# A grouped expert kernel on one core: half a unit of a visit between ScalarE's copies and the routing matmuls that read them

## The chip, the cores and the metric

The kernel runs on one core of a Trainium2 chip. Its engines are PE (TensorE, matmuls and transposes), DVE (VectorE), ACT (ScalarE), POOL (GpSimd) and SP (SyncE, which here only issues transfers). The metric is the device time of one execution in microseconds, as the median of several runs; less is better.

## The reference

A causal convolution over 7 positions with weights from a softmax makes the token rows; these are routed, by two small matmuls and two argmax, to one of 16 experts (4 groups of 4), and each token's row goes through its expert.

```python
w = softmax(weight_gen)                                # (8, 2880, 8, 7)
x = einsum('bshk,bskhg->bshg', w, windows_of(x))       # (8, 2880, 192), then 23040 rows
g_logits = x @ w_group                                 # (23040, 4)
g_idx = argmax(g_logits, axis=1); g_w = softmax(g_logits)[g_idx]
...
e_logits = xg @ w_expert[g]                            # (n, 4)
e_idx = argmax(e_logits, axis=1); e_w = softmax(e_logits)[e_idx]
...
h = maximum(xg[mask_e] @ w1[g, e], 0.0)                # 192 -> 1024
out[tok_idx] = (g_w * e_w)[:, None] * (h @ w2[g, e])   # 1024 -> 192
```

The functions `softmax` and `windows_of` stand here for the lines that the reference writes out.

## The kernel before

**Two streams in one program.** The 23040 tokens lie as 128 partitions by 180 columns, in 15 groups of 12 columns, counted from 0. The first stream makes groups: DVE convolves a group in two chunks of 6 columns (multiplications L317, additions L335), and then the group is routed. The second stream visits experts: a visit takes 128 or 256 rows of one expert through its two matmuls. Rows go from the first stream to the second through a buffer in memory: POOL scatters a group's token rows to places sorted by expert (L532, twelve scatters of 128 rows each, tensor `rows`), and SP loads a visit's rows from there (L823, tile `xb`).

**Rounds.** The visits are made in 14 rounds. Round 0 runs after groups 0 and 1, as ten short "plain" visits. Each later round r may run as soon as group r + 1 is scattered and its table of visits is made. Visits 10 to 13 belong to round 1, 14 to 18 to round 2, 19 to 25 to round 3. So visit 19 is the first that needs rows of group 4, and SP's load of its rows waits until all scatters of group 4 have landed. The last round needs the last group, 14.

**Units.** A visit is cut into units (eight hidden blocks of 128 are two in a unit). In a unit PE runs `gemm1` of that unit (L959, inputs `xh` and `xl`, weights `wa`), then `gemm2` (L1005) of the unit two before, as LAG = 2. In the first unit of a visit the next visit's rows are prepared: ScalarE copies a part of them (`xd`, L915), and in its second unit PE transposes them (tile `tpx`, L933 and L934; plain visits L922, tile `tp`) between gemm1 and gemm2; ScalarE then copies `xh` and DVE subtracts for `xl` (L890). DVE splits the weights too (`wa`, L890 as well). Units are counted here through the whole program: unit 2 is early in the plain visits, and visit 19's input transposes stand in unit 74.

**Routing a group** (`logits`, then `ranks`). ScalarE copies a part of a chunk (`rem`, L411). For each pair of columns PE makes three transposes (L418, L418, L419), and ScalarE copies them to `xT` (L424). After three pairs of each of the two chunks PE computes the scores (L401, sixteen matmuls), ScalarE copies them (L431), PE turns them (L436, the "logits' turns") and ScalarE copies `ls` (L439). DVE then finds the largest, PE counts ranks by two matmuls (L476, L477), DVE takes them over (`pre`, L487) and makes positions (`posi`, L507). For groups 2 and later POOL copies each column of posi to one of three small tiles `ix` (L531) and scatters (L532). POOL also scatters a visit's results to `out` (L1043, tiles `y`), in the one order of its instructions.

**What sets the order.** Python code writes the instructions in one order, with a clock for each engine (`clk`) that it advances by estimated costs; nothing is reordered later. The visits' loop (`blocks`) emits a unit and then calls `fill`, which lets the first stream emit steps until DVE's clock is far enough. Steps of the routing generators are taken by `move`. A generator that yields NEXT is not taken further within the unit (there is an exception in a hurry), and one that yields UNIT not before the count of gemm units has gone up. `pause(t)` yields UNIT only where the visits have begun and the copy's estimated end t lies more than 0.9 us behind PE's clock; else NEXT, after which a hurrying generator goes on in the same unit.

Of the kernel before, what the change touches and what calls it, by code (L numbers as in the profile page):

```python
# [42 lines left out]
def conv_moe_kernel(ctx: ExitStack, tc: tile.TileContext, x, wgen, w_group, w_expert, w1, w2, out):  # L43
# [205 lines left out]
        spare[name].append(spare[name].pop(0))  # L249
        return spare[name][-1]  # L250

    state = {"slots": False, "open": False, "unit": 0, "starve": False, "begun": False, "gemm": 0, "ph": 0, "hold": False}

    def ph_tile(k, shape):
        return ps_h.tile(shape, F32, name=f"ph{k}")
# [17 lines left out]
        def __init__(self, o, n):  # L273
            self.o, self.n = o, n

    NEXT, UNIT = object(), object()

    def round_of(g):
        return next(r for r in range(NR) if g < ENDS[r])
# [107 lines left out]
    def logits(g, o):  # L387
        n = WIDTHS[g]
        xrow = o.xrow
        early = g < FIRST  # L390
        pause = lambda t: UNIT if state["begun"] and t > clk["pe"] + 0.9 else NEXT
        yield Chunk(o, 1)
        new_lt = lambda: ps_y.tile([P, SG // 4, P], F32, name="py0") if g == FIRST - 1 else ps_l.tile([P, SG // 4, P], F32, name="pl")
        lt = new_lt() if early else None

        xTs = rt.tile([P, SG // 4, 2, 3, P], F32, name="xT")

        def score(q0, q1):
            for u in range(2):
                for j in range(4):  # L400
                    nc.tensor.matmul(  # L401
                        lt[j * LW:(j + 1) * LW, q0:q1, :], lhsT=wr[:, u * (1 + j % 2), :], rhs=xTs[:, q0:q1, j // 2, (j % 2, 2)[u], :],
                        start=u == 0, stop=u == 1, tile_position=(0, j * LW))

        txTs, scored = [], 0
        for s2 in range(0, n, 2):
            if o.chunks <= s2 // SC:
                yield Chunk(o, s2 // SC + 1)
            if s2 % SC == 0:
                rem = rt.tile([P, SC, HP], F32, name="rem")  # L410
                nc.scalar.copy(out=rem, in_=xrow[s2 // SC][:, :, P:D])  # L411
                txTs += [run("act", 0.4, clk["dve"])] * 2
                yield pause(txTs[-1])
            ttp = run("pe", 0.35, txTs[-2])
            tp = ps_t.tile([P, 3, P], F32, name="tp") if s2 % 4 == 0 else ph_tile(0, [P, 3, P]) if early else ps_l.tile([P, SG // 4, P], F32, name="pl")
            row = xrow[s2 // SC][:, s2 % SC:s2 % SC + 2, :]
            for u in range(2):
                nc.tensor.transpose(out=tp[:, u, :], in_=row[:, u, 0:P], identity=ident)  # L418
            nc.tensor.transpose(out=tp[:, 2, :], in_=rem[:, s2 % SC:s2 % SC + 2, :].rearrange("p s d -> p (s d)"), identity=ident)  # L419
            if early and s2 == 4:  # L420
                run("pe", 0.5, txTs[-1])
                score(0, 1)
                scored = 1
            nc.scalar.copy(out=xTs[:, s2 // 4, s2 % 4 // 2], in_=tp)  # L424
            txTs.append(run("act", 0.48, ttp))
            yield NEXT if s2 < n - 2 else pause(txTs[-1])
        lt = lt or new_lt()
        run("pe", 0.1 + 0.4 * (n // 4 - scored), txTs[-1])
        score(scored, n // 4)
        lts = xTs[:, 0].rearrange("p w u t -> p (w u) t")[:, 0:3, :]  # L430
        nc.scalar.copy(out=lts, in_=lt)  # L431
        tlt = run("act", 0.48, clk["pe"])
        yield pause(tlt)
        lp = ps_l.tile([P, SG // 4, P], F32, name="pl")
        for u in range(n // 4):
            nc.tensor.transpose(out=lp[:, u, :], in_=lts[:, u, :], identity=ident)  # L436
        run("pe", 0.35, tlt)
        ls = rt.tile([P, SG, NL], F32, name="ls")[:, 0:n, :]
        nc.scalar.copy(out=ls, in_=lp.rearrange("p q (j l) -> p (q j) l", l=LW)[:, 0:n, 0:NL])  # L439
        run("act", 0.4, clk["pe"])  # L440
        ranking.append([ranks(g, o, ls, Until(clk["act"] + LATE[0 if early else 1])), None])
# [301 lines left out]
    def move(qs, q, most):  # L743
        for _ in range(most):
            if q[1] is not None:
                what, v = q[1]
                if what == "time" and v > clk["dve"] or what == "unit" and v == state["unit"] and most < HURRY or what == "gemm" and v == state["gemm"] or what == "chunk" and (v.o.chunks < v.n or state["hold"] and v.n > 1):
                    return
                q[1] = None
            c = next(q[0], None)  # L750
# [3 lines left out]
            if c is NEXT:  # L754
                q[1] = "unit", state["unit"]
            elif c is UNIT:
                q[1] = "gemm", state["gemm"]
            elif isinstance(c, Chunk):
                q[1] = "chunk", c
            elif isinstance(c, Until):  # L760
                q[1] = "time", c
            else:
                yield c
# [3 lines left out]
    def step():  # L767
# [7 lines left out]
        if state["starve"] or not state["slots"] and c is NEXT:  # L775
            state["unit"] += 1
            state["gemm"] += state["starve"]
        return c

    def fill(until):  # L780
# [289 lines left out]
    def blocks(n0, n1, paced):  # L1070
# [99 lines left out]
        for i in range(len(units) + LAG):  # L1170
            if i < len(units):
# [14 lines left out]
                if u == last and i + 1 < len(units):  # L1186
                    cur = nxt
            asks = []
            if i >= LAG:
                b, u = queue.pop(0)  # L1190
                gemm2(b, u)
# [6 lines left out]
            if i < len(units):  # L1198
# [19 lines left out]
                    did += 1  # L1218
                state["unit"] += 1
                state["gemm"] += 1  # L1220
            flush()
            if paced:
                fill(clk["pe"] + AHEAD[0 if cur.plain else 1 if cur.o.whole else 2])
# [48 lines left out]
```

## Time and profile before

| what | value |
| --- | --- |
| median of 3 runs | 1158.08 us (1158.06 to 1162.09) |
| profiled execution | 1155.21 us |
| its span | 1153.2 us |
| PE busy | 1097.4 us, 95% |
| DVE busy | 950.2 us, 82% |
| ACT busy | 648.8 us, 56% |
| POOL busy | 583.9 us, 51% |
| moved by transfers | 275.06 MB, mean 239 GB/s |

The span is what the profiler saw between the first and the last instruction; the execution around it is 2.0 us longer, and it lies 2.9 us below the median of the other runs. A busy time is a sum over the span. An engine with less than all of it waits somewhere, and the timelines say for whom: in brackets behind an instruction stands the idle time just before it and what ended that.

### The profile page before, as it was taken

The page shows a single profiled execution, that of the slowest core. Times are in us where ns is not written, and L with a number is a line of the kernel's source. Part 1 is how long each engine was busy: PE and PEld are TensorE (multiplying, and loading weights), DVE is VectorE, ACT ScalarE, POOL GpSimd, SP SyncE. Part 2 cuts the span into 40 slices and gives each one's busy share as a digit, 9 for nine tenths or more (in the row PEclk, how much of TensorE's full clock was granted, in tenths as well). Part 3 has the DMA queues.
Part 4 walks back from the last instruction along what each step waited for, and adds up shares of the span by engine and source line. Part 5 has one row for each costly group of instructions (what it writes and reads, how often), then busy time and mean ns, then how long its engine had stood idle before and what let it go on. Part 6 is the DMA issues. An engine that isn't in the chain of part 4 may idle for free.

```text
span 1153.2 us, 23883 instructions
## 1 busy us (share of the span) xinstructions
PE 1097.4 (95%) x7909; PEld 1028.1 (89%) x7909; DVE 950.2 (82%) x1682; ACT 648.8 (56%) x1307; POOL 583.9 (51%) x613
## 2 busy tenths in 40 slices
PE   4777998999999999999999999999999999999997
PEld 2444888999999999999999999999999899999997
DVE  8899997989998999999899989899674676665661
ACT  1341444655656565565565655655656676667762
POOL 7065185738267574757484747375657321222211
PEclk9998999999999999999999999999999999999999
DMA  6798899986877887978797878875769885666562
GB/s 178 211 318 232 288 308 305 271 279 204 296 238 227 274 294 216 284 247 287 224 298 230 275 235 239 287 236 180 220 203 272 248 250 162 177 199 199 164 218 65
DMA packets 84342, 275.06 MB, mean 239 GB/s; under 512 B 15296, under 2 KB 34160, under 8 KB 82416
## 3 DMA queue, kind: packets, MB, share of 16 engines
q1 hardware_dynamic: 64056, 229.77, 64.1%
q0 software_dynamic: 20032, 43.39, 12.3%
q8 instruction: 64, 1.05, 0.4%
q14 instruction: 70, 0.57, 0.1%
q10 hardware_dynamic: 120, 0.28, 0.1%
HBM read 225.83 MB, written 47.88 MB: 237 GB/s over the span
## 4 chain that ended last, share of the span: by engine, by line
PE 73%; issue 8%; DMA 6%; DVE 6%; POOL 4%; ACT 2%; SPq 0%; POOLq 0%; DVEq 0%; ACTq 0%
PE ph L959 31%; PE py L1005 26%; PE py L1007 3%; DVE pr L317 3%; DMA raw<-in_moe_w 2%; POOL rows L532 2%; DMA xin<-in_x 2%; PE py L1008 2%; POOL out L1043 2%; PE pl L401 1%; PE tpx L934 1%; DMA xb<-rows 1%; PE tpx L933 1%; PE ph L358 1%; PE pl L1016 1%
## 5 line engine op out<-in xcount | busy, mean ns | idle before, releaser
L959 PE MATMUL ph<-xh,wa 128*128 128x256 f32 (+3 forms) x1992 | 450.6, 301 | 0.0
L1043 POOL DMA_INDIRECT out<-y,xb x189 | 217.7, 1152 | 392.3 <-DVE y L1038 164.7
L1005 PE MATMUL py<-wc,hh 128*128 128x192 f32 x2160 | 399.1, 326 | 0.0
L959 PE MATMUL ph<-xl,wa 128*128 128x256 f32 (+3 forms) x1328 | 349.8, 284 | 0.6 <-DVE xl L890 0.6
L1005 PEld LDWEIGHTS py<-wc,hh 128*128 128x128 f32 x2160 | 344.9, 189 | 0.2
L959 PEld LDWEIGHTS ph<-xh,wa 128*128 128x128 f32 x1992 | 334.2, 189 | 8.4 <-issue 8.4
L968 ACT ACTIVATE hh<-ph 128x512 f32<-128x512 f32 (+2 forms) x296 | 165.7, 560 | 252.0 <-PE ph L959 250.8
L317 DVE TENSOR_TENSOR pr<-xin,wt 128x1152 f32<-128x1152 f32 x186 | 249.0, 1350 | 4.1 <-PE py L358 3.6
L959 PEld LDWEIGHTS ph<-xl,wa 128*128 128x128 f32 x1328 | 250.7, 189 | 1.0 <-DVE xl L890 0.9
L532 POOL DMA_INDIRECT rows<-xrow,ix x156 | 222.8, 1428 | 45.8 <-POOL ix L531 34.9
L335 DVE TENSOR_TENSOR xrow<-xrow,pr 128x1152 f32<-128x1152 f32 x144 | 194.7, 1352 | 0.7
L890 DVE SCALAR_TENSOR_TENSOR pr<-ph,hh 128x256 fp32r<-128x256 f32 (+2 forms) x128 | 65.7, 513 | 81.2 <-ACT hh L973 43.1
L890 DVE TENSOR_TENSOR wa<-raw,wa 128x1024 fp32r<-128x1024 f32 x83 | 101.3, 1220 | 19.4 <-ACT wa L866 19.2
L531 POOL COPY ix<-posi 128x1 int32<-128x1 int32 x156 | 73.5, 482 | 68.3 <-DMA rows<-xrow,ix 38.3
L1007 PE MATMUL py<-wc,hh 128*128 128x384 f32 x320 | 101.1, 361 | 0.0
L973 ACT ACTIVATE hh<-ph 128x256 fp32r<-128x256 f32 (+2 forms) x128 | 59.1, 462 | 53.7 <-PE ph L959 53.6
L866 ACT CAST wa<-raw 128x1024 fp32r<-128x1024 f32 x83 | 87.1, 1050 | 0.0
L875 ACT CAST wa<-raw 128x1024 fp32r<-128x1024 f32 x83 | 86.5, 1042 | 0.0
L1008 PE MATMUL py<-wc,pr 128*128 128x192 f32 x320 | 80.1, 250 | 0.0
L1032 ACT ACTIVATE y<-py,xb 128x192 f32<-128x192 f32 x175 | 66.2, 426 | 21.1 <-PE py L1005 19.4
L890 DVE TENSOR_TENSOR xl<-tpx,xh 128x512 fp32r<-128x512 f32 (+1 forms) x83 | 56.4, 680 | 14.3 <-ACT xh L939 14.0
L1008 PEld LDWEIGHTS py<-wc,pr 128*128 128x128 f32 x320 | 60.9, 190 | 0.0
(205 smaller groups left out, 1315.6 us busy)
## 6 DMA issues: line engine op xcount, KB each, us to landing
wc<-in_moe_w SPq DMA_DIRECT2D x73, 768.0 KB, 6.5
raw<-in_moe_w SPq DMA_DIRECT2D x83, 512.0 KB, 6.1
xin<-in_x SPq DMA_DIRECT2D x14, 1728.0 KB, 10.8
raw<-in_moe_w SPq DMA_DIRECT2D x91, 256.0 KB, 5.2
raw<-w1lo SPq DMA_DIRECT2D x83, 256.0 KB, 5.2
xb<-rows SPq DMA_DIRECT2D x75, 194.0 KB, 5.1
wa<-in_moe_w SPq DMA_DIRECT2D x24, 384.0 KB, 6.7
raw<-in_moe_w SPq DMA_DIRECT2D x11, 768.0 KB, 8.6
```

What stands on the lines that cost most here:

```text
L317: nc.vector.tensor_tensor(out=dst, in0=o.xin[:, c0 + k:c0 + k + SC, :].rearrange("p s (h g) -> p s h g", g=HG), in1=w4[:, c0:c0 + SC, :, k ...
L335: nc.vector.tensor_tensor(out=acc, in0=acc, in1=prs[k - 2], op=ALU.add)
L532: written_once(nc.gpsimd.indirect_dma_start(out=rows[:, :], out_offset=bass.IndirectOffsetOnAxis(ap=ix, axis=0), in_=src, in_offset=None, ...
L866: nc.scalar.copy(out=o.wa[:, 0, :], in_=o.raw[0])
L875: nc.scalar.copy(out=o.wa[:, 2, :], in_=o.raw[1])
L890: f(*a, **k)
L959: nc.tensor.matmul(ph[:, v, :], lhsT=w[:, f0:f0 + P], rhs=rhs, start=i == 0, stop=i == len(terms) - 1)
L968: nc.scalar.activation(out=hh, in_=ph, func=AF.Relu)
L1005: nc.tensor.matmul(b.acc[t], lhsT=hh[:, v, c], rhs=wc[0][:, f, :], start=f == 0 and not (b.wide and t == 1), stop=f == NFT - 1 and not (b. ...
L1007: nc.tensor.matmul(b.py[t], lhsT=hh[:, v, c], rhs=wc[f // 4][:, f % 4].rearrange("p l d -> p (l d)"), start=f == 0, stop=False)
L1008: nc.tensor.matmul(b.acc[t], lhsT=hl[:, v, c], rhs=wc[f // 4][:, f % 4, 0, :], start=False, stop=f == NFT - 1)
L1043: ins = nc.gpsimd.indirect_dma_start(out=out[:, :], out_offset=bass.IndirectOffsetOnAxis(ap=b.x.bitcast(I32)[part, t, D + 1:D + 2], axis=0 ...
```

## The change

Between gemm1 and gemm2 of a unit there is now a point at which a routing generator can go on. A new count, `half`, goes up at that point and again at the unit's end; a generator that yields HALFWAY isn't taken further until the count has gone up. `brief(t)` yields HALFWAY for groups below MAIN + 3 = 6, if the visits have begun, and for the last group; for others it is `pause(t)` as before. It stands in two places: after the last transposes, before the scores, and after the scores, before the turns. If a generator waits for a half, `fill` is called at the new point as well.

```diff
@@ -249,7 +249,7 @@
-    state = {"slots": False, "open": False, "unit": 0, "starve": False, "begun": False, "gemm": 0, "ph": 0, "hold": False}
+    state = {"slots": False, "open": False, "unit": 0, "starve": False, "begun": False, "gemm": 0, "half": 0, "ph": 0, "hold": False}
@@ -273,7 +273,7 @@
-    NEXT, UNIT = object(), object()
+    NEXT, UNIT, HALFWAY = object(), object(), object()
@@ -389,6 +389,7 @@
         pause = lambda t: UNIT if state["begun"] and t > clk["pe"] + 0.9 else NEXT
+        brief = lambda t: HALFWAY if state["begun"] and (g < MAIN + 3 or g + 1 == ENDS[-1]) else pause(t)
@@ -423,14 +424,14 @@
             txTs.append(run("act", 0.48, ttp))
-            yield NEXT if s2 < n - 2 else pause(txTs[-1])
+            yield NEXT if s2 < n - 2 else brief(txTs[-1])
         lt = lt or new_lt()
         run("pe", 0.1 + 0.4 * (n // 4 - scored), txTs[-1])
         score(scored, n // 4)
         lts = xTs[:, 0].rearrange("p w u t -> p (w u) t")[:, 0:3, :]
         nc.scalar.copy(out=lts, in_=lt)
         tlt = run("act", 0.48, clk["pe"])
-        yield pause(tlt)
+        yield brief(tlt)
@@ -744,7 +745,7 @@
-                if what == "time" and v > clk["dve"] or what == "unit" and v == state["unit"] and most < HURRY or what == "gemm" and v == state["gemm"] or what == "chunk" and (v.o.chunks < v.n or state["hold"] and v.n > 1):
+                if what == "time" and v > clk["dve"] or what == "unit" and v == state["unit"] and most < HURRY or what == "gemm" and v == state["gemm"] or what == "half" and v == state["half"] or what == "chunk" and (v.o.chunks < v.n or state["hold"] and v.n > 1):
@@ -755,6 +756,8 @@
             elif c is UNIT:
                 q[1] = "gemm", state["gemm"]
+            elif c is HALFWAY:
+                q[1] = "half", state["half"]
@@ -775,6 +778,7 @@
             state["gemm"] += state["starve"]
+            state["half"] += state["starve"]
@@ -1186,6 +1190,9 @@
             asks = []
+            state["half"] += 1
+            if paced and any(q[1] and q[1][0] == "half" for q in scoring):
+                fill(clk["pe"] + AHEAD[0 if cur.plain else 1 if cur.o.whole else 2])
             if i >= LAG:
@@ -1218,6 +1225,7 @@
                 state["gemm"] += 1
+                state["half"] += 1
```

Below is what stands in a row on three engines. The changed kernel's line numbers are a few higher (L401 is L402, L436 is L437, L959 is L963, L1005 is L1009, L890 is L894, L531 is L532, L532 is L533, L1043 is L1047).

On PE, group 4's second chunk. Before, in unit 52: the end of a gemm2, the transposes (`xrow`, `rem`), the scores into `pl`, the turns, then the next gemm1:

```order
L1005 MATMUL py_2429<-wc,hh 128x192
L418 MATMUL pl<-ident,xrow 128x128 x2
L419 MATMUL pl<-ident,rem 128x128
L418 MATMUL tp<-ident,xrow 128x128 x2
L419 MATMUL tp<-ident,rem 128x128
L418 MATMUL pl<-ident,xrow 128x128 x2
L419 MATMUL pl<-ident,rem 128x128
L401 MATMUL pl<-xT,wr 32x384 x8
L436 MATMUL pl<-ident,xT 128x128 x3
L959 MATMUL ph_2503<-xh_181,wa 128x256 x2
```

After, from the last transposes of unit 54 to the first matmuls of unit 56:

```order
L419 MATMUL pl<-ident,xrow 128x128 x2
L420 MATMUL pl<-ident,rem 128x128
...
L963 MATMUL ph_2561<-xh_181,wa 128x256
L963 MATMUL ph_2561<-xl_183,wa 128x256
L402 MATMUL pl<-xT,wr 32x384 x8
L1009 MATMUL py_2586<-wc,hh 128x192
L1009 MATMUL py_2587<-wc,hh 128x192
L1009 MATMUL py_2586<-wc,hh 128x192
L1009 MATMUL py_2587<-wc,hh 128x192
L437 MATMUL pl<-ident,xT 128x128 x3
L963 MATMUL ph_2611<-xh_181,wa 128x256 x2
```

The transposes stand two units later, in a unit that also holds a visit's input transposes; a gemm1 has moved between them and the scores, and a gemm2 between the scores and the turns. Groups 2, 3 and 14 change in the same way: the second transposes of 2 and 14 stay in their unit (2 and 271), those of 3 go from 27 to 28, and the scores of each stand behind the next unit's gemm1. Group 4's rank matmuls move from unit 57 to 60, those of group 2 from 10 to 11, of group 3 from 33 to 35, of group 14 from 274 to 276. In group 5, which already had a gemm2 between its transposes and its scores in unit 77, the scores move ahead of that gemm2, and the turns from unit 78 to the end of 77; its first transposes move from unit 66, which holds input transposes, to 67. Group 4's first transposes move from unit 43 to 46, which holds input transposes.

On DVE, the same group from the ranks to the positions. Before:

```order
L335 TENSOR_TENSOR xrow<-xrow,pr 128x6x192
L317 TENSOR_TENSOR pr<-xin,wt 128x1152
L487 COPY pre<-pl 128x16x11
...
L501 TENSOR_TENSOR sel<-sel,oh 128x192
L890 TENSOR_TENSOR wa<-raw_193,wa 128x1024
L890 TENSOR_TENSOR xl_183<-tpx,xh_181 128x2x256
L504 TENSOR_REDUCE pos<-sel 128x12
L507 SCALAR_TENSOR_TENSOR posi<-pos 128x12
```

After:

```order
L894 TENSOR_TENSOR wa<-raw_193,wa 128x1024
L894 TENSOR_TENSOR xl_183<-tpx,xh_181 128x2x256
...
L335 TENSOR_TENSOR xrow<-xrow,pr 128x6x192 x2
L288 TENSOR_REDUCE m<-wt 128x96
L290 TENSOR_TENSOR wt<-wt,m 128x672
L488 COPY pre<-pl 128x16x11
...
L502 TENSOR_TENSOR sel<-sel,oh 128x192
L505 TENSOR_REDUCE pos<-sel 128x12
L508 SCALAR_TENSOR_TENSOR posi<-pos 128x12
```

The subtractions wa and xl have left the middle of the chain and stand ahead of it; the pair of additions and two operations of the next softmax, which stood behind posi, are ahead of `pre` now. In the last group wa and xl move from before `pre` to a place earlier still, ahead of the group's second argmax.

On POOL, the same group's scatters. Before, an out scatter and the first rows of the chain, whose twelve scatters have nothing between them:

```order
L1043 DMA out<-y_187,xb 23040x192
L531 COPY ix_177<-posi 128x1
L531 COPY ix_178<-posi 128x1
L531 COPY ix_176<-posi 128x1
L532 DMA rows<-xrow,ix_177 188928x194
L532 DMA rows<-xrow,ix_178 188928x194
L532 DMA rows<-xrow,ix_176 188928x194
L531 COPY ix_177<-posi 128x1
L532 DMA rows<-xrow,ix_177 188928x194
```

After, from the third scatter on:

```order
L533 DMA rows<-xrow,ix_176 188928x194
L532 COPY ix_177<-posi 128x1
L1047 DMA out<-y_188,xb 23040x192
L533 DMA rows<-xrow,ix_177 188928x194
L532 COPY ix_178<-posi 128x1
L532 COPY ix_176<-posi 128x1
L1047 DMA out<-y_189,xb 23040x192
L533 DMA rows<-xrow,ix_178 188928x194
L533 DMA rows<-xrow,ix_176 188928x194
```

Two out scatters that stood behind the chain stand inside it. On SP two row loads move: visit 14's stands behind a weight load (`wc`) that it stood ahead of, and visit 19's behind three (`raw`).

## Rows read from the trace of the kernel before

**Rows 1.** The page: busy time of the engines, share of the span, instructions.

```profile
PE 1097.4 (95%) x7909; PEld 1028.1 (89%) x7909; DVE 950.2 (82%) x1682; ACT 648.8 (56%) x1307; POOL 583.9 (51%) x613
```

**Rows 2.** Stretch 165 to 215 us: busy time, clock, DMA share, GB/s.

```profile
165.00:215.00 50.00, 44.41 (x335) 41.05 (x334) 42.86 (x80) 26.95 (x57) 31.99 (x32) 1.00 1.03 317
```

**Rows 3.** Waits of PE, 105 to 300 us: total us, times, longest us.

```profile
PE pl L436 <- ACT xT L431: 1.8, 3, 0.6
PE pl L401 <- ACT xT L424: 1.7, 3, 0.6
PE tp L922 <- DMA xb<-rows: 1.7, 1, 1.7
...
PE tpx L933 <- DMA xb<-rows: 1.3, 1, 1.3
```

**Rows 4.** Timeline of PE, group 4: start, us, operation, [idle before <-releaser].

```profile
229.58 0.44 PE L418 MATMUL pl<-ident,xrow 128*128 128x128 f32 x2 [0.24 <-ACT xT L424]
...
230.69 1.50 PE L401 MATMUL pl<-xT,wr 128*32 128x384 f32 x16 [0.57 <-ACT xT L424]
232.79 0.55 PE L436 MATMUL pl<-ident,xT 128*128 128x128 f32 x3 [0.60 <-ACT xT L431]
```

**Rows 5.** Waits of PE, 820 to 930 us.

```profile
PE tpx L933 <- DMA xb<-rows: 1.2, 2, 0.9
PE pl L436 <- ACT xT L431: 0.6, 1, 0.6
PE pl L401 <- ACT xT L424: 0.6, 1, 0.6
```

**Rows 6.** Timeline of PE, 245 to 291 us: ranks, two units, transposes, v19.

```profile
245.92 0.25 PE L476 MATMUL pl<-oh,tri 128*128 128x192 bf16 x1
...
246.03 0.48 PE L959 MATMUL ph<-xh,wa 128*128 128x256 f32 x2
...
253.84 0.54 PE L959 MATMUL ph<-xh,wa 128*128 128x256 f32 x2
...
271.73 0.44 PE L418 MATMUL tp<-ident,xrow 128*128 128x128 f32 x2 [1.17 <-ACT xT L424]
...
290.96 0.27 PE L933 MATMUL tpx<-ident,xb 128*128 128x128 f32 x1
```

**Rows 7.** Timeline of DVE, group 4's positions and the convolution behind them.

```profile
250.33 0.17 DVE L507 SCALAR_TENSOR_TENSOR posi<-pos 128x12 int32<-128x12 f32 x1
...
253.74 2.75 DVE L335 TENSOR_TENSOR xrow<-xrow,pr 128x1152 f32<-128x1152 f32 x2
```

**Rows 8.** Timeline of POOL: an out scatter, then group 4's chain.

```profile
250.87 0.98 POOL L1043 DMA_INDIRECT out<-y,xb  x1 [0.30 <-ACT wa L875]
...
254.99 0.97 POOL L532 DMA_INDIRECT rows<-xrow,ix  x1 [0.30 <-issue]
258.21 1.11 POOL L531 COPY ix<-posi 128x1 int32<-128x1 int32 x1 [2.25 <-DMA rows<-xrow,ix]
...
278.96 1.80 POOL L532 DMA_INDIRECT rows<-xrow,ix  x1 [0.28 <-POOL ix L531]
```

**Rows 9.** Timeline of SP: the row load of visit 19.

```profile
283.73 0.33 SPq L823 DMA_DIRECT2D xb<-rows  x1
```

**Rows 10.** Timeline of PE, last group: ranks, unit 277, first stalled visit.

```profile
845.14 0.25 PE L476 MATMUL pl<-oh,tri 128*128 128x192 bf16 x1
...
850.12 0.42 PE L959 MATMUL ph<-xh,wa 128*128 128x256 f32 x1
...
895.66 0.33 PE L933 MATMUL tpx<-ident,xb 128*128 128x128 f32 x1 [0.85 <-DMA xb<-rows]
```

**Rows 11.** Timeline of DVE, last group: from the ranks to the positions.

```profile
848.93 0.33 DVE L487 COPY pre<-pl 128x176 f32<-128x176 f32 x1
...
851.35 0.17 DVE L507 SCALAR_TENSOR_TENSOR posi<-pos 128x12 int32<-128x12 f32 x1
```

**Rows 12.** Timeline of SP: the load that PE waits for at 895.66.

```profile
893.29 0.33 SPq L823 DMA_DIRECT2D xb<-rows  x1
```
## The prediction

> **What bounds the kernel now.** I read the page first, then the windows, PE's waits, and the timelines around each wait. The page shows PE busy for 95% of the span [rows 1], so only time in which PE stands still can be won, and each such time has a releaser. In the list of PE's waits between 105 and 300 us the reader is to see two pairs: the scores (L401) wait three times for ScalarE's copy L424, the logits' turns (L436) three times for the copy L431 [rows 3]. These are groups 2, 3 and 4 (counted from 0); the timeline of group 4 shows one pair, 0.57 and 0.60 us [rows 4]. The last group pays it once more [rows 5]. The other waits in these lists are for rows that come back from memory (xb) [rows 3, 5]. Between 165 and 215 us the DMA engines are booked for 1.03 of the time and PE's granted clock is 1.00 [rows 2], so PE's time lost there is lost to transfers.
>
> **What the change removes.** Today the transposes, the copy, the scores, the copy and the turns of a group stand in one unit, and PE waits out both copies. Now gemm1 of the next unit stands over the first copy and its gemm2 over the second. PE's work is the same, so the gain is the wait itself: 0.57 + 0.60 = 1.17 us for each group that pays. For groups 2 to 4 that is 1.8 + 1.7 = 3.5 us [rows 3], for the last group 0.6 + 0.6 = 1.2 [rows 5]; 4.7 us in all, an upper bound, as group 5's waits are not in the list of pairs. Cover: a copy and its hop take 0.57 to 0.60 us, and a unit's gemm1 and gemm2 together fill some 2.5 us (three units with one set of input transposes take 253.84 - 246.03 = 7.81 us [rows 6]), so either half is longer than the copy, unless the copy is queued behind other work of ScalarE.
>
> **What it moves among the transposes.** Group 4's second transposes move from unit 52 to unit 54, behind the input transposes of the next visit. There ScalarE has that visit's copies first: the same situation now costs 1.17 us for group 5 at unit 66 [rows 6], against 0.24 for group 4 at unit 52 [rows 4]. That is 0.93 lost. Group 5's first transposes leave unit 66 for 67, which has no input transposes: 0.93 won. I take these two as cancelling. Group 4's first transposes move from unit 43 to 46 as well; I take nothing, between nothing and 1.17 lost.
>
> **What is late next, group 3.** PE's waits for rows at 183 and 191 us (1.7 and 1.3 us [rows 3]) lie in the stretch whose DMA share is 1.03 [rows 2]. A PE that comes 1.17 us earlier waits 1.17 us longer there if the transfers keep their times. Bounds: nothing absorbed, or both group 2's and group 3's gains (2.34). I take group 3's alone, since its gain arises inside this stretch and group 2's before it, where loads follow PE's releases.
>
> **What is late next, group 4.** Its rank matmuls move from unit 57 to unit 60, three units or 7.81 us [rows 6]. PE is then 1.17 + 1.17 - 0.93 = 1.41 us early, so they start at 245.92 + 7.81 - 1.41 = 252.3. From the copy `pre` to `posi` the last group needs 851.35 - 848.93 = 2.4 us with nothing between [rows 11]; with 0.3 for the ranks and 0.2 for posi itself that is 255.2. On DVE the subtractions wa and xl no longer stand inside this chain, but the L335 pair of 2.75 us [rows 7] and two softmax operations now stand ahead of it; I take 255.5, bounds 254 (group 3's gain kept) and 256.5. Today posi starts at 250.33 [rows 7], and POOL begins the chain at 250.87 + 0.98 = 251.85, behind an out scatter [rows 8]: 3.65 us later now.
>
> The chain of twelve scatters ends at 278.96 + 1.80 = 280.76 [rows 8], so it lasts 28.9 us. Two out scatters now stand inside it, 0.98 + 0.30 us each [rows 8]: 2.56 more; some of it can hide in the pause of 2.25 us that an index copy spends on a scatter's buffer [rows 8], so between 0 and 2.56; I take all, as the outs stand behind the paused copy. The end: 255.5 + 28.9 + 2.56 = 287.0. SP issues visit 19's rows at 283.73 [rows 9], 2.97 after the chain. The last group shows 895.66 - 893.29 = 2.37 us from issue to the waiting transpose [rows 10, 12]. So the rows are usable at 287.0 + 2.97 + 2.37 = 292.3. PE reads them at 290.96 today with no wait [rows 6], and would be there 1.17 + 1.17 = 2.34 us earlier, at 288.6 (group 5's 0.93 has come back by then). A new wait of 3.7 us: PE is 1.3 us behind today from there. Behind this transpose PE queues gemm2 and group 5's transposes, ScalarE queues a weight cast and the copy `rem` behind xd of the same rows, and DVE the subtraction xl. On SP three weight loads now stand ahead of this row load instead of behind it; SP waits for the scatters anyway, so I take nothing.
>
> **What is late next, last group.** Its ranks move from unit 274 to the end of unit 276. That is 850.1 today [rows 10], less 1.2 for its own waits, plus the 1.3 carried in: 850.2, and pre follows 0.3 later, at 850.5 against 848.93 [rows 11], since wa and xl now run before it. The scatters, and the load at 893.29 [rows 12], follow by 1.5. PE would be at that visit at 895.66 - 0.85 + 1.3 - 1.2 = 894.9 and waits until 897.2, 1.5 us behind today's 895.66 [rows 10]. The 1.2 us won here are given back.
>
> **Sum.** -3.5 (groups 2 to 4) + 1.2 (group 3 absorbed) + 3.7 (visit 19), then -1.2 + 1.3 (last group): +1.5 us. The profiled execution took 1155.2, so 1156.7; it lies 2.9 us below the median of the runs, 1158.1, and by that median I predict 1159.6. A difference under 0.5%, 5.8 us, is about what a measurement of this kernel cannot tell from none.
>
> **A page weighed against a row.** The chain's length is the open number. One scatter takes 0.97 us while two L335 additions run on DVE (254.99 to 255.96, inside 253.74 to 256.49), another takes 1.80 [rows 7, 8]. The Trainium skill, SBUF - State Buffer, section "SBUF: two separate sides", has a DVE operation with two SBUF inputs hold the port pair that it shares with GpSimd for its whole length, while a GpSimd operation that reads SBUF stands blocked. By that rule every scatter beside the convolution is a slow one, and the sum would be the third rival's. The scatter at 254.99 speaks against it, the one at 278.96 does not.
>
> **Rivals.** (1) The forecast, gains and new wait within 0 to +3 us: 1158.1 to 1161. Chance 0.45. (2) The gains of the early groups stay. If group 3's is kept, the ranks come 1.2 earlier and the out scatters hide, the rows are usable at 292.3 - 0.3 - 1.2 - 2.6 = 288.2 against a need at 287.4: a wait of 0.8, and -2.7 + 0.1 for the last group, 1155.5; with no wait at all some 1154.6. For it speaks the pause of 2.25 us, against it that everything must fall well. 1154.6 to 1158: 0.24. (3) The other side, one mechanism: visit 19's chain is slow from end to end. Seven of its scatters are near 0.97 today; at 1.80 each the chain is 7 x 0.83 = 5.8 us longer, and PE 7.3 behind: 1165.4. It counts as slower from some five slow scatters more (4.3 + 1.5 = 5.8). For it speaks that the chain starts 3.65 us later, so more of it lies where the slow ones lie today. Chance 0.22 for over +3, of which 0.09 over 5.8. (4) The change doesn't do what it says: the copies stand behind others on ScalarE and PE waits as long as before. Then nothing is won and the ranks of group 4 still come later, by 1.4 us more than above: rows at 293.7 against 290.96, +2.7, some 1161: 0.07. The remaining 0.02 is for an effect elsewhere.
>
> **How the numbers follow.** The upper bound of the gain, 4.7 us, is less than 5.8, so faster by over 0.5% has 0.03; slower has the slow chain's 0.09 and 0.01 of the rest; the same 0.87. The range 1155.0 to 1163.0 holds the forecast, nearly all of (2), (4) and the first half of (3). The likeliest case's own range is 1158.1 to 1161.
>
> **What the profile after would show.** Right: no waits at the scores and turns of groups 2, 3, 4 and the last; longer waits for xb at 182 and 190 us by about 1.2; posi of group 4 near 255.5 and a POOL chain with two outs inside ending near 287; a new wait of PE of 2 to 5 us for visit 19's rows near 289; in the last group the wait for xb at 895 up by some 1.5. Wrong: no wait at visit 19 (then the chain is shorter or its load is not tied to its end), waits at 182 and 190 unchanged (group 3 kept), or scores that still wait for L424.

## The result and the profile after

| | before | changed |
| --- | --- | --- |
| median | 1158.9 us (1153.5 to 1170.3, 22 runs) | 1164.6 us (1158.8 to 1175.7, 22 runs) |
| ratio | | 1.0056, 95% interval 1.0039 to 1.0073 |
| profiled execution, span | 1155.2, 1153.2 us | 1163.9, 1161.9 us |

The change makes the kernel slower by 0.56%, some 6.5 us (5.7 by the medians); I had forecast 1159.6 in a range of 1155.0 to 1163.0, so it is outside. The profile after, beginning with the page's row of busy times, which answers to [rows 1]:

```profile
PE 1104.6 (95%) x7909; PEld 1035.8 (89%) x7909; DVE 951.6 (82%) x1682; ACT 648.9 (56%) x1307; POOL 574.2 (49%) x613
```

Of the 8.7 us by which the span grew, PE's busy time holds 7.2, with the same number of instructions. The same matmuls took longer; waiting alone doesn't do that. (Of the 8.7 us, 3.6 stand ahead of unit 1, and of the 7.2 us 2.8; nothing is changed there, and profiles differ among themselves.) PE's waits from 105 to 300 us, and below them those from 820 to 930 us (total, times, longest), as in [rows 3, 5]:

```profile
PE tp L926 <- DMA xb<-rows: 5.5, 1, 5.5
PE tpx L937 <- DMA xb<-rows: 3.3, 2, 3.0
PE tpx L358 <- DVE pr L353: 2.4, 2, 1.7
PE tp L419 <- ACT xT L425: 1.7, 3, 1.2
PE pl L419 <- ACT xT L425: 1.4, 2, 1.2
```

```profile
PE tpx L937 <- DMA xb<-rows: 2.5, 1, 2.5
PE pl L419 <- ACT xT L425: 0.2, 1, 0.2
```

The waits of the scores and of the turns are gone, all eight of them, as the change intends. In their place stand longer waits for rows: 5.5 us instead of 1.7 at unit 34, 3.0 where there was none, 2.5 instead of 0.9 near the end; the 1.3 us at unit 38 are gone. The timeline of PE at group 4 shows the halves at work, scores and turns without a bracket, and the price among the transposes that the prediction named, 1.17 instead of 0.24 [rows 4]:

```profile
241.61 0.44 PE L419 MATMUL pl<-ident,xrow 128*128 128x128 f32 x2 [1.17 <-ACT xT L425]
...
243.24 1.50 PE L402 MATMUL pl<-xT,wr 128*32 128x384 f32 x16
246.07 0.49 PE L437 MATMUL pl<-ident,xT 128*128 128x128 f32 x3
```

Group 4's first transposes, for which the prediction took nothing, now wait 1.17 us as well (the 1.2 in the row of `tp` and L419 above), against 0.94 before. So PE's idle time at group 4's routing between units 34 and 58 is 2.34 us, and it was 2.35: what is won at the scores and turns is paid at the transposes, and comes back at group 5's.

The timeline of PE from the new wait to the next unit, at visit 19:

```profile
298.46 0.33 PE L937 MATMUL tpx<-ident,xb 128*128 128x128 f32 x1 [2.98 <-DMA xb<-rows]
298.90 0.47 PE L938 MATMUL tpx<-ident,xd 128*128 128x128 f32 x1
299.17 0.42 PE L937 MATMUL tpx<-ident,xb 128*128 128x128 f32 x1
299.38 0.42 PE L938 MATMUL tpx<-ident,xd 128*128 128x128 f32 x1
299.59 2.73 PE L1009 MATMUL py<-wc,hh 128*128 128x192 f32 x8
302.15 0.38 PE L419 MATMUL pl<-ident,xrow 128*128 128x128 f32 x2
302.37 0.27 PE L420 MATMUL pl<-ident,rem 128*128 128x128 f32 x1
302.40 0.48 PE L963 MATMUL ph<-xh,wa 128*128 128x256 f32 x2
```

The gemm2 behind the wait, eight matmuls, takes 2.73 us. From the first input transpose to the next unit it is 3.94 us. In the kernel before the same eight take 1.47, and the next unit starts 1.99 us after the transposes at 290.96 [rows 6]:

```profile
291.40 1.47 PE L1005 MATMUL py<-wc,hh 128*128 128x192 f32 x8
...
292.95 0.48 PE L959 MATMUL ph<-xh,wa 128*128 128x256 f32 x2
```

The windows say why: PE's granted clock (the number behind the busy times) falls to 0.76 around this wait, and to 0.59 behind the one at unit 34, between the two levels of 1.2 and 2.4 GHz. The third row is the kernel before, around visit 19, with a clock of 1.00:

```profile
188.00:194.00 6.00, 5.79 (x28) 5.62 (x29) 0.71 (x5) 2.10 (x4) 0.97 (x1) 0.59 1.05 250
296.00:303.00 7.00, 4.43 (x20) 4.16 (x21) 6.86 (x7) 3.80 (x8) 3.45 (x4) 0.76 0.91 278
288.00:296.00 8.00, 8.00 (x62) 7.96 (x61) 7.27 (x7) 5.89 (x11) 4.07 (x4) 1.00 1.03 364
```

At unit 34 the difference is not the change's alone. With the last group only, where nothing is moved up to there, PE waits 1.9 us at unit 34 instead of 1.7 and its clock is 0.58 from 183 to 187 us; yet units 34 to 58 take 65.6 us against 65.3, as the wait at unit 38 is gone. So a fall of the clock in this stretch need not cost time.

**A table by stages.** Unit 1 starts between 113.4 and 117.2 us in the profiles, though nothing ahead of it is changed, so single profiles are compared from there. Each number is the difference between the starts of two units (the first gemm1 row of each in PE's timeline), in us; "wait" is PE's idle time at the input transposes of that unit.

| kernel | 1 to 34 | 34 to 58 | 58 to 75 | 75 to 300 | sum | wait 34 | wait 74 | ratio |
| --- | --- | --- | --- | --- | --- | --- | --- | --- |
| before | 67.1 | 65.3 | 46.9 | 619.1 | 798.4 | 1.7 | 0 | |
| changed | 64.4 | 69.6 | 51.2 | 618.7 | 803.9 | 5.5 | 3.1 | 1.0056 |
| changed, again | 64.4 | 68.8 | 52.8 | 620.1 | 806.0 | 4.2 | 4.5 | |
| early groups only | 64.4 | 66.6 | 52.3 | 619.5 | 802.8 | 4.1 | 4.4 | 1.0047 |
| last group only | 67.1 | 65.6 | 46.9 | 619.4 | 799.1 | 1.9 | 0 | 0.9982 |
| without group 4 | 64.4 | 71.8 | 51.5 | 618.7 | 806.4 | 3.7 | 3.3 | 1.0019 |
| fill waits | 64.4 | 71.9 | 52.5 | 620.5 | 809.3 | 4.4 | 2.1 | 1.0035 |
| late ranks alone | 67.1 | 64.5 | 50.3 | 625.7 | 807.5 | 1.4 | 1.9 | 1.0048 |
| group 4 and last | 67.1 | 66.3 | 47.6 | 619.4 | 800.5 | 3.2 | 0.1 | 0.9997 |
| fill more | 64.4 | 66.0 | 53.0 | 620.0 | 803.4 | 0 | 2.1 | 1.0060 |
| outs behind | 64.5 | 67.5 | 47.7 | 618.1 | 797.9 | 3.7 | 1.2 | 1.0004 |
| work ahead of transfers | 69.5 | 63.4 | 46.9 | 619.5 | 799.4 | 0 | 0 | 1.0022 |
| group 4, last, outs behind | 67.1 | 64.7 | 47.1 | 618.9 | 797.8 | 2.2 | 0 | 0.9987 |

The reader is to see three things. The gain at groups 2 and 3 is real, 2.7 us up to unit 34, in every kernel that has their halves, and the next column takes back a part of it or more (that column differs by up to 3 us between profiles of the same code). The loss stands in the column 58 to 75, 4.3 to 5.8 us in the changed kernel and its early part. And one edit takes nearly all of that away ("outs behind").

### The profile page after: what moved, and what is told of

Its sections match the earlier page's. It is cut to its first block, busy times and chain, and to the rows that moved or that the text cites. A ratio compares the mean times of both kernels' runs of the same rounds, so it can differ in the third digit from the quotient of the medians.

```text
span 1161.9 us, 23880 instructions
## 1 busy us (share of the span) xinstructions
PE 1104.6 (95%) x7909; PEld 1035.8 (89%) x7909; DVE 951.6 (82%) x1682; ACT 648.9 (56%) x1307; POOL 574.2 (49%) x613
## 4 chain that ended last, share of the span: by engine, by line
PE 76%; issue 8%; DVE 6%; DMA 5%; POOL 3%; ACT 1%; SPq 0%; POOLq 0%; DVEq 0%; ACTq 0%
PE ph L963 32%; PE py L1009 27%; PE py L1011 4%; DVE pr L317 3%; DMA xb<-rows 3%; PE py L1012 2%; PE pl L402 2%; POOL out L1047 1%; PE tpx L938 1%; PE tpx L937 1%; PE ph L358 1%; POOL rows L533 1%; DVE pr L353 1%; PE pl L1020 1%; PE tp L419 1%
## 5 line engine op out<-in xcount | busy, mean ns | idle before, releaser
L963 PE MATMUL ph<-xh,wa 128*128 128x256 f32 (+3 forms) x1992 | 451.6, 302 | 0.0
L1047 POOL DMA_INDIRECT out<-y,xb x189 | 211.8, 1121 | 399.7 <-ACT y L1036 165.3
L1009 PE MATMUL py<-wc,hh 128*128 128x192 f32 x2160 | 402.2, 328 | 0.0
L963 PE MATMUL ph<-xl,wa 128*128 128x256 f32 (+3 forms) x1328 | 350.5, 285 | 0.6 <-DVE xl L894 0.6
L1009 PEld LDWEIGHTS py<-wc,hh 128*128 128x128 f32 x2160 | 347.3, 191 | 3.2 <-issue 3.1
L963 PEld LDWEIGHTS ph<-xh,wa 128*128 128x128 f32 x1992 | 335.3, 190 | 7.8 <-issue 7.8
L963 PEld LDWEIGHTS ph<-xl,wa 128*128 128x128 f32 x1328 | 251.5, 189 | 1.0 <-DVE xl L894 0.9
L533 POOL DMA_INDIRECT rows<-xrow,ix x156 | 225.4, 1445 | 49.0 <-POOL ix L532 36.8
L894 DVE SCALAR_TENSOR_TENSOR pr<-ph,hh 128x256 fp32r<-128x256 f32 (+2 forms) x128 | 65.8, 514 | 81.6 <-ACT hh L977 43.9
L894 DVE TENSOR_TENSOR wa<-raw,wa 128x1024 fp32r<-128x1024 f32 x83 | 101.3, 1221 | 14.3 <-ACT wa L870 14.1
L532 POOL COPY ix<-posi 128x1 int32<-128x1 int32 x156 | 68.3, 450 | 74.3 <-DMA rows<-xrow,ix 37.3
L1036 ACT ACTIVATE y<-py,xb 128x192 f32<-128x192 f32 x175 | 66.3, 425 | 22.9 <-PE py L1009 20.8
L894 DVE TENSOR_TENSOR xl<-tpx,xh 128x512 fp32r<-128x512 f32 (+1 forms) x83 | 56.5, 681 | 14.9 <-ACT xh L943 14.4
```

Source lines behind the costliest of these rows:

```text
L533: written_once(nc.gpsimd.indirect_dma_start(out=rows[:, :], out_offset=bass.IndirectOffsetOnAxis(ap=ix, axis=0), in_=src, in_offset=None, ...
L894: f(*a, **k)
L963: nc.tensor.matmul(ph[:, v, :], lhsT=w[:, f0:f0 + P], rhs=rhs, start=i == 0, stop=i == len(terms) - 1)
L1009: nc.tensor.matmul(b.acc[t], lhsT=hh[:, v, c], rhs=wc[0][:, f, :], start=f == 0 and not (b.wide and t == 1), stop=f == NFT - 1 and not (b. ...
L1047: ins = nc.gpsimd.indirect_dma_start(out=out[:, :], out_offset=bass.IndirectOffsetOnAxis(ap=b.x.bitcast(I32)[part, t, D + 1:D + 2], axis=0 ...
```

## The experiments

The theory after the result (A): PE's new waits for rows cost more than their length, as the clock falls behind them; the wait at visit 19 comes from group 4's late ranks and lengthened chain of scatters. The rival (B): the waits cost their length, and the rest of the loss is in the last group or elsewhere. The edits are to the changed kernel, unless "the kernel before" is said.

**Where is the loss?** The early groups alone, the last group alone, and all but group 4:

```diff
-        brief = lambda t: HALFWAY if state["begun"] and (g < MAIN + 3 or g + 1 == ENDS[-1]) else pause(t)
+        brief = lambda t: HALFWAY if state["begun"] and g < MAIN + 3 else pause(t)
...
+        brief = lambda t: HALFWAY if state["begun"] and g + 1 == ENDS[-1] else pause(t)
...
+        brief = lambda t: HALFWAY if state["begun"] and g != 4 and (g < MAIN + 3 or g + 1 == ENDS[-1]) else pause(t)
```

> Only groups 2 to 5 use the halves; the last group is as before. Theory A (each of the two new long waits for rows, before visits 9 and 19, costs its length and then some 2 us more in which PE runs at the lower clock): nearly all of the loss is here, +4 to +7 us against the kernel before, the granted clock falls below 0.9 behind both waits, and the sum of PE's busy time is some 5 us above that of before. Theory B (only the waiting itself costs, and the rest of the loss seen is in the last group): +1 to +3 us, PE's busy time as before.

Measured: 1.0047 (1.0023 to 1.0072), +5.4 us by the ratio: the loss is in the early groups, as A expects. PE's busy time in the profile is 1101.3 us, 3.9 above before, not 5.

> Only the last group uses the halves; nothing is moved before unit 271. Theory A: the first 830 us are as before, the wait for rows near 895 us is 1 to 2 us longer with a short fall of the clock behind it, total 0 to +2 us. Theory B (the loss is mostly the last group's): +3 to +5 us.

Measured: 0.9982 (0.9962 to 1.0001). The last group costs nothing, so B falls where it puts the loss there. The table shows a zero sum there: 1.6 us less from unit 75 to 273, and the wait near 895 us grows from 1.0 to 3.3, 3.2 of it in this row of the waits:

```profile
PE tpx L937 <- DMA xb<-rows: 3.2, 1, 3.2
```

> As the changed kernel, but group 4 is taken without halves, as before. Its ranks then stand in unit 58 instead of 60. If the late ranks of group 4 are what makes PE wait for visit 19 (my prediction's step), that wait is gone or under 1 us and the total is 3 to 5 us less than that of the changed kernel, +1 to +3 us against before. If the wait comes from elsewhere (the transfers, the order of loads on SP) it stays at about 3 us and the total too.

Measured: 1.0019 (1.0002 to 1.0036) by the ratio, 4.0 us by the medians, and in its profile the wait at visit 19 is still 3.3 us. So an earlier rank (unit 58) alone does not remove the wait: posi comes 7.3 us after the start of unit 58 instead of 11.8, but from there the chain takes 35.9 us instead of 31.4, and so ends no earlier. As POOL's timeline shows, two out scatters stand in this kernel's chain too, further back, ahead of its last three scatters:

```profile
281.33 1.80 POOL L533 DMA_INDIRECT rows<-xrow,ix  x1 [0.28 <-DMA raw<-in_moe_w]
283.43 0.97 POOL L1047 DMA_INDIRECT out<-y,xb  x1 [0.30 <-issue]
284.40 0.47 POOL L532 COPY ix<-posi 128x1 int32<-128x1 int32 x1
285.02 1.98 POOL L1047 DMA_INDIRECT out<-y,xb  x1 [0.15 <-ACT wa L870]
287.31 2.13 POOL L533 DMA_INDIRECT rows<-xrow,ix  x1 [0.30 <-issue]
```

It was a poor experiment for its question, since it changed two things. Its scatters and outs take as long as in the changed kernel (20.4 and 20.3 us in sum); the chain is longer by what stands between them, and what made that longer is not shown.

**Late ranks alone.** The kernel before, group 4's ranks in unit 60:

```diff
-        yield NEXT
+        yield from (NEXT,) + (UNIT,) * (2 if g == 4 else 0)
         t12 = ps_l.tile([P, 2, SG * NE], F32, name="pl")[:, :, 0:n * NE]
```

> The kernel before with one edit: group 4's rank matmuls are held back by two more units, so that they stand in unit 60 as in the changed kernel, with two out scatters inside POOL's chain; no half is used, every copy wait stays. If the late ranks make the loss at visit 19 (my prediction's step), a wait of 4 to 6 us for its rows appears at unit 74, with the slow clock behind it (some 1.8 us), and the time is 5 to 8 us above before; the waits at units 34 and 38 stay as in before. If the loss comes from elsewhere, the time is within 1.5 us of before.

Measured: 1.0048 (1.0021 to 1.0075). The wait appears, with the slow clock behind it (4.0 us from the transposes to the next unit), but it is 1.9 us, not 4 to 6: posi came 10.8 us after unit 58's start, against 11.8 in the changed kernel. A second wait stands at unit 122, 1.7 us, where neither the kernel before nor the changed one has one, and units 75 to 300 take 6.6 us more than before; so its total is no clean measure of the ranks.

**Group 4 and the last group.**

```diff
+        brief = lambda t: HALFWAY if state["begun"] and (g == 4 or g + 1 == ENDS[-1]) else pause(t)
```

> Only group 4 and the last group use the halves. Group 4's ranks then move by one unit (57 to 58) and no out scatter comes into its chain. If the late ranks and not the halves cost the time, there is no wait at unit 74, units 34 to 46 are as before, 1.2 us are won at group 4 and 0 to 1.2 at the last group: 1 to 2.5 us less than before. If halves cost by themselves, the time is 1 to 3 us above before.

Measured: 0.9997 (0.9977 to 1.0016): no loss, and no gain that can be told. The wait at unit 74 is 0.1 us. My expectation had no out scatter in the chain; on the chip two stand in it here as well, ahead of its last three scatters as in the kernel without group 4. Its chain takes 32.9 us from posi, against 35.9 there, and PE comes to visit 19 about 0.8 us later after the start of unit 58, as group 5's transposes still wait. So two outs in the chain don't make the wait by themselves; with the ranks early enough they fit.

**Two out scatters.** The changed kernel, with the two out scatters held behind group 4's last scatter by a dependency. No row on PE, DVE, ACT or SP moves:

```diff
+        if g == 4:
+            state["pin"] = 2
...
+        if state.get("pin"):
+            state["pin"] -= 1
+            tc.add_manual_dep(ins.ins, state["last"].ins.name, mybir.DependencyInfo(mybir.DependencyClass.NoSync, mybir.DependencyReason.DATA), reason="behind the rows")
```

`state["last"]` is the scatter issued last in `scatter_row`, `ins` an out scatter.

> The changed kernel with one edit: the two out scatters that stand inside group 4's chain are held behind its last scatter; nothing else moves on any engine. If the length of that chain sets PE's wait at visit 19, the wait of 3 to 4.5 us falls by 2.6 us to 0.5 to 2, units 58 to 75 take 48 to 50 us instead of 51 to 53, and the time falls by 2 to 4.5 us against the changed kernel (to +1 to +4 us above before; more than 2.6 if the slow clock goes with the wait). If the chain is not what PE waits for, nothing changes.

Measured: 1.0004 (0.9985 to 1.0023), 1157.2 us against 1157.6. Taking 2.6 us out of POOL's chain (30.3 to 27.7 us from the first scatter to the last) takes the whole measured loss away. SP's three weight loads stand ahead of the row load here too, so their order is not what cost the time. The waits, and PE's timeline at visit 19:

```profile
PE tpx L940 <- DMA xb<-rows: 1.1, 1, 1.1
```

```profile
293.72 0.33 PE L940 MATMUL tpx<-ident,xb 128*128 128x128 f32 x1 [1.08 <-DMA xb<-rows]
294.16 0.33 PE L941 MATMUL tpx<-ident,xd 128*128 128x128 f32 x1
294.32 0.27 PE L940 MATMUL tpx<-ident,xb 128*128 128x128 f32 x1
```

The wait falls to 1.1 us and the transposes behind it run at their usual 0.11 us from one to the next; units 58 to 75 take 47.7 us against 51.2 to 52.8. That is 3.5 to 5.0 us for an edit of 2.6: the slow clock went with the wait. The mean granted clock over its runs is 0.990, against 0.988 in the changed kernel. A page bears on this: the Trainium skill, TensorE: Matmul & The Clock Gate, section "HAM oscillation — how this bites in real kernels", tells of waits for transfers after which PE starts its next work at the lower clock. The trace agrees, with 2.73 us against 1.47.

**What a wait costs.** The kernel before, with waits where it has none:

```diff
+MORE = {26: 7, 34: 10, 42: 13, 50: 18}
...
+        for _ in range(1 + MORE.get(b.k, 0)):
+            nc.scalar.copy(out=b.xd, in_=b.x[:, :, P:D].unsqueeze(2).broadcast_to([P, b.nt, 2, HP]))
```

`b.k` is the visit's number.

> The kernel before, in which ScalarE makes the copy xd of visits 26, 34, 42 and 50 not once but 8, 11, 14 and 19 times (0.3 us each), so that PE has to wait at units 102, 134, 166 and 198, where it never waits. It measures what a wait costs by itself. If a wait costs its length only, the unit takes longer by the wait and not more. If the lower clock follows, waits of some 2 us and more are followed by 1.5 to 2 us in which matmuls take twice as long, and short ones are not. In all some 8 to 16 us above before.

Measured: 1.0174 (1.0137 to 1.021), some 20 us, above my 8 to 16. The unit with the wait and what follows, in its profile, against the same units before (behind the last three, the next unit is 0.1, 0.1 and 0.4 longer as well):

| unit | wait | unit longer by | beyond the wait |
| --- | --- | --- | --- |
| 102 | 2.92 | 2.77 | none |
| 134 | 2.83 | 4.62 | 1.8 |
| 166 | 3.81 | 5.48 | 1.7 |
| 198 | 6.34 | 8.01 | 1.7 |

PE's timeline at the first and at the second of them, and the windows around the second to fourth:

```profile
373.18 0.33 PE L936 MATMUL tpx<-ident,xd 128*128 128x128 f32 x1 [2.92 <-ACT xd L917]
...
373.56 1.47 PE L1007 MATMUL py<-wc,hh 128*128 128x192 f32 x8
```

```profile
463.18 0.33 PE L936 MATMUL tpx<-ident,xd 128*128 128x128 f32 x1 [2.83 <-ACT xd L917]
...
463.63 2.77 PE L1007 MATMUL py<-wc,hh 128*128 128x192 f32 x8
```

```profile
463.00:467.00 4.00, 3.82 (x16) 3.73 (x17) 2.73 (x3) 3.44 (x8) 3.44 (x6) 0.57 0.35 69
558.00:563.00 5.00, 3.79 (x16) 3.79 (x17) 2.72 (x7) 4.01 (x10) 0.24 (x1) 0.66 0.14 20
653.00:658.00 5.00, 3.90 (x15) 3.90 (x16) 2.98 (x3) 3.72 (x9) 4.16 (x7) 0.50 0.33 75
```

So a wait can have a surcharge of about 1.8 us here, not in proportion to its length, and not each time: of two waits of the same length one was followed by the lower clock and one not.

**Filling the waits.** 26, 24 and 16 transposes that nobody reads ahead of the input transposes of visits 9, 19 and 73, then 44, 40 and 24:

```diff
+FILLER = {9: 26, 19: 24, 73: 16}
...
+            for _ in range(FILLER.get(b.k, 0)):
+                nc.tensor.transpose(out=tpv[:, 0, 0:P], in_=ident, identity=ident)
```

> As the changed kernel, but PE makes transposes of the identity that nobody reads (26, 24 and 16 of them) right ahead of the input transposes of visits 9, 19 and 73, where it would stand still. Theory A: the waits stay, but the granted clock doesn't fall behind them, and the time falls by 3 to 5 us against the changed kernel, to +1 to +3 us against before. Theory B: the clock plays no part, and the time is that of the changed kernel or up to 2 us more.

> As the run that fills the waits, with 44, 40 and 24 transposes ahead of visits 9, 19 and 73, so that hardly any of the standing still is left. If PE's slow clock behind the waits costs some 2 us each, the units behind the waits (35 to 36, 74) run at their usual length (1.55 and, from the input transposes to the next unit, 2.0 us instead of 3.8), and the time is 2 to 5 us under the changed kernel. If filling does nothing for the clock, those units stay long and the time is that of the changed kernel.

Measured: 1.0035 (1.0018 to 1.0052) and 1.0060 (1.0036 to 1.0084). Where the filler reached the end of the wait, the clock stayed up: with 44 transposes the gemm1 behind the wait at unit 34 is back at its usual length (1.06 us for eight matmuls, against 1.91 in the changed kernel). The mean granted clock over all runs rose to 0.992, above that of before (0.991) and of the changed kernel (0.988). But the time did not fall as I expected. In the profile with more filler the rows of visit 19 were issued 3.7 us after the chain's end instead of 1.6, and PE waited 2.1 us behind 4.5 us of filler; whether the filler has to do with that, or overran shorter waits in other runs, these runs don't settle. A slow clock that is avoided was not time won, so that the surcharge is shown in the profiles and by the waits made by hand, not by taking it away.

**The transfers.** The kernel before, with 11 unread transposes each at units 14 and 30:

```diff
+            for _ in range(11 if b.k in (4, 8) else 0):
+                nc.tensor.transpose(out=tp[:, 0, :], in_=ident, identity=ident)
```

> The kernel before, with 11 transposes that nobody reads ahead of the input transposes of visits 4 and 8 (units 14 and 30), 2.4 us of PE's time in all, as much as the change wins at groups 2 and 3. If the transfers between 165 and 215 us set the time and not PE, units 1 to 34 take 2.4 us longer and units 34 to 40 as much less, and the time stays as before (within 1.5 us): what is lost ahead of the transfers is nothing lost, and so what is won there is nothing won. If PE sets the time, it is 2.4 us more.

Measured: units 1 to 34 take 2.4 us longer (69.5), the wait at unit 34 is gone, and units 34 to 58 take 1.9 less (63.4): in this profile the stretch takes back a loss ahead of it, and the profile's sum is 0.9 above before. The runs don't bear that out. Their ratio, 1.0022 (1.0005 to 1.004), is +2.5 us (0.6 to 4.6), above my bound of 1.5 us and where the rival, that PE sets the time, put it (2.4). So the profile and the runs disagree, and that the transfers set the time there is not shown by this experiment.

**A second look, and the best of the parts.**

> The changed kernel once more, for a second profile. If the waits at units 34 (3.7 to 5.5 us) and 74 (about 3 to 4.5 us) are the change's own they are there again; the time at which unit 1 starts may differ by some us, since nothing ahead of it has changed.

Measured: 1165.1 us; waits of 4.2 and 4.5 us, unit 1 at 115.0 us instead of 117.2. The two waits are the change's own, the start is not.

> Only group 4 and the last group use the halves, and the two out scatters of group 4's chain are held behind it. Group 4's ranks stand in unit 58. If the chain and its length were all that went against the change there, PE has no wait at unit 74, units 58 to 75 take 46.9 us as before, the 1.2 us won at group 4 stay, and the time is 1 to 3 us less than before; at units 294 to 300 the last group's 1.2 us are given back as in the other runs. If the early transfers and the clock decide instead, the time is within 1 us of before.

Measured: 0.9987 (0.9964 to 1.001), 1157.2 against 1158.4 us. No wait at unit 74, units 58 to 75 at 47.1. The sign is as expected, but the interval holds no change; no version here is shown to beat the kernel before.

## Why the prediction was wrong

**The waits removed: right.** All eight are gone, and up to unit 34 the gain is 2.7 us (2.34 forecast; PE's idle time there fell by 2.34). Group 4's own gain was paid at its transposes: its first ones, put at nothing, cost 0.23 beside the 0.93 of the second.

**Group 2's and 3's gain in the stretch of transfers: half right.** The step that failed is "I take group 3's alone, since its gain arises inside this stretch". From unit 1 to unit 58 the changed kernel took 134.0, 133.2, 131.0 and 132.0 us (the early groups alone and the outs behind have the same work on PE up to there) against 132.4, 132.7 and 132.6 in the profiles with the code of before (the second and third are the last group alone and the waits by hand). On average that is no difference, where I had 1.4 less. So the upper bound that I gave, all 2.34 absorbed, is nearer than the term; with a spread of 3.0 us its size is rough, and what absorbed it, the transfers or the clock behind the wait at unit 34, stays open, as the runs with work ahead of the transfers went the other way.

**Group 4's chain: right in place, and in size with some luck.** The step put posi 10.9 us after unit 58's start, the chain at 31.5 and the way to PE at 5.3, so PE at 47.7. The rows of unit 58, posi, the two outs, the last scatter, and SP's load:

```profile
251.19 0.42 PE L963 MATMUL ph<-xh,wa 128*128 128x256 f32 x1
```

```profile
263.03 0.17 DVE L508 SCALAR_TENSOR_TENSOR posi<-pos 128x12 int32<-128x12 f32 x1
```

```profile
264.08 1.62 POOL L533 DMA_INDIRECT rows<-xrow,ix  x1 [0.39 <-POOL ix L532]
...
269.83 0.98 POOL L1047 DMA_INDIRECT out<-y,xb  x1 [0.16 <-issue]
...
273.80 1.79 POOL L1047 DMA_INDIRECT out<-y,xb  x1 [0.16 <-issue]
...
292.60 1.80 POOL L533 DMA_INDIRECT rows<-xrow,ix  x1 [0.28 <-POOL ix L532]
```

```profile
295.99 0.34 SPq L827 DMA_DIRECT2D xb<-rows  x1
```

That is 11.8 to posi, 31.4 from there to the chain's end, 4.1 from there to the transposes at 298.46: 47.3, and 48.7 in the second profile. The wait of 3.7 us that I forecast is 3.1 and 4.5. Two errors cancel in the first profile: posi came 0.9 us later than forecast, and the way from the chain to PE was 1.2 shorter.

**What that wait costs: wrong.** The step that failed is "A new wait of 3.7 us: PE is 1.3 us behind today from there". It prices a wait at its length. Units 58 to 75 should have been 2.8 us longer (3.7 less the 0.93 won at group 5's transposes) and are 4.3 and 5.8, and 5.4 with the early groups alone. Of the difference, about 1.9 us is the lower clock (3.9 us from the transposes to the next unit against 2.0). I read the clock in the rows, but only where PE had not yet waited so long. (The runs with filler kept the clock up and were not faster, so this 1.9 us stands on the profiles.) My third rival, slower by a longer chain, had the right place and side, but its mechanism, all scatters at 1.80 us, isn't what happened: the chain took 31.4 and 32.6 us from posi, for 31.5 in the forecast. (Before, six of its scatters were near 0.97 and one took 1.30; I counted seven.)

**The last group: right.** Its 1.2 us are won and given back.

**The sum.** About nothing up to unit 58 for my -1.4, +5.2 (the mean of three) from 58 to 75 for +2.8, and about nothing behind it for +0.1: +5.2, inside the ratio's interval (+6.5, 4.5 to 8.5). The bound of 0.5%, from which I call a change slower, was passed by a little.

A sentence of the opening sections has to be mended: it says that nothing is reordered after the Python code. On POOL the rows stand otherwise than the code writes them (three copies ahead of three scatters, out scatters between, where the code writes copy and scatter twelve times in one loop without a yield), and a dependency could move two of them alone. A scheduler stands between: the kernel's `manual_schedule` names PE, ACT, DVE and SP, not POOL. It put the two out scatters into the chain.

## What to carry to other kernels

Ask of a moved step not only what it waits for but who waits at the end of its chain, and look for strangers in that chain: with the ranks as late as the change puts them, two out scatters on POOL's queue were worth its whole loss, and more than the eight waits on PE that it removed. Weigh a new wait of PE with a surcharge for the clock behind it: here about 1.8 us, behind nearly all waits of 2.2 us and more and behind few of less than 1.5 us. Don't count what PE wins ahead of a stretch in which the DMA share is above 1.0 before you have looked behind that stretch: in these profiles it was gone there.

## What the runs showed of the hardware

PE's lower clock comes behind waits of very different length, and not behind each: behind 1.9 us in the kernel with late ranks, not behind 2.9 us in one of the waits made by hand. Where it came in the waits made by hand, it cost about 1.8 us, whether the wait was 2.8 or 6.3 us; at unit 34 with the last group alone it cost next to nothing. In all the profiles together, from unit 1 to 930 us, the granted clock fell behind 19 of the 21 waits of 2.2 us and more (not behind 2.92 and 3.19), behind 8 of the 12 of 1.6 to 2.2 us, and behind shorter ones of 1.0 to 1.5 us at two places only, where a second wait followed within 2 us. Keeping PE busy with work that nobody reads kept the clock up (0.992 in the mean of the runs) and yet left the time as it was. How many scatters are slow says little of a chain's length: with the outs behind, eight of twelve took over 1.4 us, against five before, and the chain 27.7 us against 28.3, as its pauses were shorter. No chain of group 4 was as slow as the third rival has it: its 5.8 us and the outs' 2.56 on top of 28.3 are 36.7 us from the first scatter, and the longest, without group 4's halves, took 34.9, more by its pauses than by slow scatters (six).
